# Attention and feed-forward on one core: value products in bursts, three shared PSUM buffers, and transposes on PE straight from the loaded rows

## The chip, the cores and the metric

The kernel runs on one core of a Trainium2 chip. The metric is the device time in microseconds (us), median of several runs. Engines: PE multiplies matrices, DVE (VectorE) and ACT (ScalarE) do elementwise work, POOL and SP mostly issue DMAs.

## The reference, cut to what matters

```python
# q, k, v: (8, 12, 448, 64)   w_in: (768, 2048)   w_out: (2048, 768)
scores = q @ k.T / sqrt(64)                  # for each batch and head
attn   = maximum(scores, 0) ** 2 / 448
x      = (attn @ v), heads side by side      # (8*448, 768)
out    = gelu(x @ w_in) @ w_out              # exact gelu
```

There is no softmax: each score tile goes through ReLU and a square, then into the value products. The first feed-forward layer is called F1 below and the second F2. Four heads are a "quad"; three quads make a batch.

## The kernel before

The core of attention: a score step fills one of two PSUM buffers (two banks each), ACT empties it, DVE squares it, and a value step accumulates into two further banks, which the quad holds from its first value step to its last copy.

```python
s_pp = pool("s_pp", 2, PS); av_pp = pool("av_pp", 2, PS); f_pp = pool("f_pp", 2, PS)

def qk_step(b, g, i):                        # 4 matmuls, 64x64 tiles, 448 columns
    ps = s_pp.tile([128, 2, NB], F32, tag="s", name="ps")
    ...
    nc.scalar.activation(ar, ps[:, :, :S], AF.Relu, scale=c_att)
    nc.vector.tensor_mul(a2, ar, ar)

def av_step(b, g, i):                        # 4 matmuls; i of 7 steps
    if i == 0:
        pav[b, g] = [av_pp.tile([128, NB], F32, tag="av", name="pav") for j in range(2)]
    ...
    if i == NK - 1:
        for j in range(2):
            nc.vector.tensor_copy(xT[b][:, 2 * g + j, :], pav[b, g][j][:, :S])
```

Rows of q and k have to be transposed before they can be multiplied. Batches 0 to 2 are first permuted by DVE, then transposed by PE; later batches are permuted by DVE and transposed by DMA. The tiles that hold the loaded rows (`nq`, `nk`) have one buffer each, so a batch can be loaded only when the one before it has been read.

```python
def transpose_dma(b):
    for w in (1, 0):
        ...
            nc.sync.dma_start_transpose(get_T(b)[w][:, :, off : off + r], perm[b][w][:r, t, :])

for b in range(2, B):                        # steady part
    ...
    if b == 2:
        prep[2] = [later(quad_T, 2, 1)]      # batch 2's quads: transposes on PE
        prep[6] = [later(quad_T, 2, 2)]
    if b + 1 < B:
        nxt = [later(permute_k, b + 1), later(permute_q, b + 1), later(transpose_dma, b + 1)]
    l = 10 if b == 2 else 2
    prep[l] = nxt
    if b + 2 < B:
        prep[l + 8] = [later(load, b + 2, 0, G)]
    weave(todo, atoms, prep)                 # two score steps, two value steps, some F1/F2
```

## Time and profile before

| | before |
|---|---|
| time, median of 3 | 423.77 us |
| span of the profiled run | 421.0 us |
| PE, DVE, ACT busy | 94%, 44%, 51% |
| first F1 product | 41.25 us |
| first F2 product | 87.99 us |
| from the last F2 product to the end | about 5 us |

### The profile page before, as it was taken

The page shows a single profiled execution, that of the slowest core. Times are in us where ns is not written, and L with a number is a line of the kernel's source. Part 1 is how long each engine was busy: PE and PEld are TensorE (multiplying, and loading weights), DVE is VectorE, ACT ScalarE, POOL GpSimd, SP SyncE. Part 2 cuts the span into 40 slices and gives each one's busy share as a digit, 9 for nine tenths or more (in the row PEclk, how much of TensorE's full clock was granted, in tenths as well). Part 3 has the DMA queues.
Part 4 walks back from the last instruction along what each step waited for, and adds up shares of the span by engine and source line. Part 5 has one row for each costly group of instructions (what it writes and reads, how often), then busy time and mean ns, then how long its engine had stood idle before and what let it go on. Part 6 is the DMA issues. An engine that isn't in the chain of part 4 may idle for free.

```text
span 421.0 us, 7489 instructions
## 1 busy us (share of the span) xinstructions
PE 395.6 (94%) x3152; PEld 200.8 (48%) x3152; DVE 186.1 (44%) x330; ACT 213.3 (51%) x302; POOL 60.9 (14%) x94
## 2 busy tenths in 40 slices
PE   2958998999989999999999999999999999999995
PEld 1323444554545545545445455545455455555562
DVE  1776656336446444464455443463453543300121
ACT  4875665654553556456564565465564654223200
POOL 8363060404104100050005000000000000000000
PEclk9998999999999999999999999999999999999998
DMA  9999399974995990199516990162011111001122
GB/s 141 159 156 200 63 164 209 205 117 78 174 191 85 172 173 15 39 140 166 99 37 92 179 174 2 39 142 66 2 37 39 39 37 29 24 26 37 39 75 75
DMA packets 68417, 41.41 MB, mean 98 GB/s; under 512 B 36640, under 2 KB 64800, under 8 KB 68384
## 3 DMA queue, kind: packets, MB, share of 16 engines
q0 software_dynamic: 35280, 22.58, 38.7%
q1 hardware_dynamic: 33104, 18.36, 22.3%
q8 instruction: 24, 0.39, 0.4%
q14 instruction: 9, 0.07, 0.1%
HBM read 45.61 MB, written 11.01 MB: 135 GB/s over the span
## 4 chain that ended last, share of the span: by engine, by line
PE 87%; DVE 5%; ACT 4%; issue 2%; DMA 1%; POOL 0%; ACTq 0%; DVEq 0%; POOLq 0%
PE pso L227 35%; PE psh L211 34%; PE pav L192 9%; PE ps L172 7%; ACT a_relu L180 4%; PE tp L144 2%; DVE a_sq L182 2%; DMA nk<-in_k_dram 1%; DVE xT L203 1%; DVE qT L150 1%; DVE kT L150 0%; DVE pk L132 0%; DVE pq L126 0%; POOL nk L79 0%; DVE osb L235 0%
## 5 line engine op out<-in xcount | busy, mean ns | idle before, releaser
L180 ACT ACTIVATE a_relu<-ps 128x896 bf16<-128x896 f32 x168 | 144.7, 916 | 116.6 <-PE ps L172 116.6
L211 PE MATMUL psh<-xT,win_sb 128*128 128x448 bf16 x768 | 156.6, 353 | 0.0
L227 PE MATMUL pso<-wout_sb,h_sb 128*128 128x384 bf16 x896 | 152.8, 326 | 0.0
L182 DVE TENSOR_TENSOR a_sq<-a_relu 128x896 bf16<-128x896 bf16 x168 | 104.4, 624 | 91.0 <-ACT a_relu L180 90.6
L227 PEld LDWEIGHTS <-h_sb 128*128 128x128 bf16 x896 | 86.3, 98 | 63.1 <-issue 5.9
L211 PEld LDWEIGHTS <-win_sb 128*128 128x128 bf16 x768 | 70.5, 98 | 79.4 <-issue 19.7
L218 ACT ACTIVATE h_sb<-psh 128x448 bf16<-128x448 f32 x128 | 70.0, 547 | 60.9 <-PE psh L211 60.9
L235 DVE COPY osb<-pso 128x384 f32<-128x384 f32 x56 | 31.2, 558 | 110.3 <-PE pso L227 110.3
L192 PE MATMUL pav<-a_sq,v_sb 64*64 64x448 bf16 x672 | 53.8, 370 | 10.0 <-DVE a_sq L182 5.2
L172 PE MATMUL ps<-qT,kT 64*64 64x448 bf16 x672 | 51.9, 368 | 4.1 <-ACT a_relu L180 2.8
L203 DVE CAST xT<-pav 128x448 bf16<-128x448 f32 x48 | 27.7, 619 | 16.2 <-PE pav L192 16.2
L192 PEld LDWEIGHTS <-v_sb 64*64 64x64 bf16 x672 | 16.3, 107 | 38.7 <-issue 36.9
L79 POOL DMA_DIRECT2D nk<-in_k_dram x12 | 9.4, 783 | 149.8 <-DVE pk L133 139.3
L89 POOL DMA_DIRECT2D v_sb<-in_v_dram x48 | 29.0, 628 | 14.3 <-DMA nk<-in_k_dram 8.9
L172 PEld LDWEIGHTS <-kT 64*64 64x64 bf16 x672 | 21.2, 108 | 20.6 <-issue 9.3
L144 PE MATMUL tp<-ident,pq 112*128 112x112 bf16 x72 | 6.2, 241 | 5.6 <-ACT pq L329 5.6
L83 POOL DMA_DIRECT2D nq<-in_q_dram x11 | 9.5, 859 | 0.7 <-DMA nk<-in_k_dram 0.5
L132 DVE COPY pk<-nk 128x768 bf16<-128x768 bf16 (+1 forms) x14 | 7.1, 510 | 5.4 <-DMA nk<-in_k_dram 5.4
L144 PE MATMUL tp<-ident,pk 128*128 128x128 bf16 x72 | 8.6, 232 | 0.4 <-DVE pk L132 0.4
L80 POOL DMA_DIRECT2D nk<-in_k_dram x12 | 8.4, 703 | 3.5 <-DMA win_sb<-in_moe_w_in_dram 3.5
L144 PEld LDWEIGHTS <-pk 128*128 128x128 bf16 x72 | 5.5, 101 | 5.5 <-DVE a_sq L182 1.2
L144 PEld LDWEIGHTS <-pq 112*128 112x128 bf16 x72 | 4.5, 112 | 7.4 <-ACT pq L329 5.6
(18 smaller groups left out, 32.8 us busy)
## 6 DMA issues: line engine op xcount, KB each, us to landing
v_sb<-in_v_dram POOLq DMA_DIRECT2D x48, 112.0 KB, 13.6
nq<-in_q_dram POOLq DMA_DIRECT2D x6, 672.0 KB, 14.8
win_sb<-in_moe_w_in_dram POOLq DMA_DIRECT2D x4, 768.0 KB, 10.2
wout_sb<-in_moe_w_out_dram POOLq DMA_DIRECT2D x2, 1536.0 KB, 16.9
out_dram<-osb SPq DMA_DIRECT2D x8, 336.0 KB, 2.8
nk<-in_k_dram POOLq DMA_DIRECT2D x6, 384.0 KB, 7.1
out_dram<-osb SPq DMA_DIRECT2D x8, 288.0 KB, 2.6
out_dram<-osb SPq DMA_DIRECT2D x8, 240.0 KB, 2.8
```

Source lines behind the costliest of these rows:

```text
L83: nc.gpsimd.dma_start(nq[b][:, h0:h1, :], qq)
L89: nc.gpsimd.dma_start(vt[b][64 * j : 64 * j + 64, g], vv[g, j])
L144: nc.tensor.transpose(tp[:, j, off : off + r], perm[b][w][:r, t, bass.ts(2 * g + j, 128)], ident[:r, :r],)
L172: nc.tensor.matmul(ps[64 * j : 64 * j + 64, e, :S], kT[r, 2 * g + j, kcol(i) : kcol(i) + KB], qT[r, 2 * g + j, :], start=True, stop=True,)
L180: nc.scalar.activation(ar, ps[:, :, :S], AF.Relu, scale=c_att)
L182: nc.vector.tensor_mul(a2, ar, ar)
L192: nc.tensor.matmul(pav[b, g][j][64 * e : 64 * e + 64, :S], vt[b][r, g, e, bass.ts(i, D)], a2[r, e, :], start=(i == 0), stop=(i == NK - 1),)
L203: nc.vector.tensor_copy(xT[b][:, 2 * g + j, :], pav[b, g][j][:, :S])
L211: nc.tensor.matmul(ph[:, :S], win_sb[:, kd, bass.ts(m, 128)], xT[b][:, kd, :], start=(kd == 0), stop=(kd == KD - 1),)
L218: nc.scalar.activation(hT[b // 2][:, m, (b % 2) * S : (b % 2 + 1) * S], ph[:, :S], AF.Gelu)
L227: nc.tensor.matmul(po[:, :ND], hT[pr][:, kf, bass.ts(t, 128)], wout_sb[:, kf, bass.ts(n, ND)], start=(kf == 0), stop=(kf == KF - 1),)
L235: nc.vector.tensor_copy(osb[:, bass.ts(n, ND)], po[:, :ND])
```

## The change

The intent: fewer changes between attention and feed-forward on PE, and an earlier start. The value products of a quad run as one burst of 28 matmuls; scores and values share three PSUM buffers of two banks; batches 0 to 2 are transposed by PE straight from the loaded rows, without DVE's permutation. With this come a planner that fixes each engine's order of work from estimated durations, batch 0 in two halves of q, ReLU on ACT or DVE while the first two batches run, and dummy matmuls at the start. Cut to its core:

```diff
-    s_pp = pool("s_pp", 2, PS)
-    av_pp = pool("av_pp", 2, PS)
+    w_pp = pool("w_pp", 3, PS)
     f_pp = pool("f_pp", 2, PS)
...
+        def fn(e_):                                   # values of one quad
+            pav.append(w_pp.tile([128, 2, NB], F32, tag="w", name="pav"))
+            for i, x in enumerate(blocks):            # 7 steps x 4 matmuls, one burst
...
+        def fn(e):                                    # transposes of k, no permutation
+            for i in range(NK):
+                for e in range(2):
+                    nc.tensor.transpose(
+                        tp[64 * e : 64 * e + 64, bass.ts(i, 128)],
+                        nk[b][:, 2 * g + e, bass.ts(i, D)], ident)
...
+            op = sch.add((("SP", 0.9, 12.0),), fn, [Pk[b, g]] + ...)  # DMA transpose, as planned
...
+    def slots(todo, first):                           # AV + 2 QK, or 3 QK, per slot
+            slot, room = [], first if not out else 3
...
+    for _ in range(SPIN):                             # SPIN = 45 dummies
+        nc.tensor.matmul(spin[:, 0, :128], zero, zero, start=True, stop=True)
...
+    add_win(0)
+    add_q(0, 0, G, HC, NC)                            # second half of q, batch 0
+    add_win(1)
...
+    add_steps(halves(0), dve=True)
...
+            n = per * (b - 2) + (6 if b == 2 else 0)  # copies of batch b + 1: after slot n
+            add_pk(b + 1, 0, G, after=at(n))
+            add_pq(b + 1, 0, G, after=at(n))
+            add_T_dma(b + 1, ...)
...
+    prep = {1: t2[1], 4: t2[2]}                       # batch 2's quads 1 and 2: slots 1 and 4
+    pe_q.extend(t2[0])
```

## The prediction

> **What bounds the kernel now.** I first read busy time by stretch, cutting where the work changes: the load, attention of batch 0 alone (to 41 us), attention of batch 1 with the first feed-forward products (to 78), the steady mixture (to 361), feed-forward alone. Columns: us, PE, PEld, DVE, ACT, POOL busy (instructions), clock, DMA share, GB/s.
>
> ```profile
> 0.00:6.00 6.00, 0.37 (x5) 0.37 (x6) 0.12 (x2) 2.53 (x3) 4.90 (x12) 1.00 0.75 137
> 6.00:20.00 14.00, 11.36 (x99) 4.76 (x96) 8.17 (x19) 9.65 (x12) 6.51 (x11) 1.00 1.16 162
> 20.00:41.00 21.00, 14.25 (x174) 6.42 (x173) 16.07 (x32) 14.07 (x17) 10.90 (x17) 0.92 1.20 171
> 41.00:78.00 37.00, 33.79 (x300) 16.35 (x293) 21.75 (x44) 24.64 (x36) 12.62 (x18) 1.00 0.97 155
> 78.00:361.00 283.00, 281.08 (x2269) 141.67 (x2267) 131.00 (x220) 153.75 (x219) 25.98 (x38) 1.00 0.59 93
> 361.00:421.00 60.00, 54.80 (x324) 31.23 (x320) 8.97 (x16) 8.70 (x16) 0.00 (x0) 0.98 0.16 46
> ```
>
> After 78 us PE never rests (281.08 of 283.00), and DVE and ACT are half idle: only PE's own work counts there. Before 41 us all engines have gaps: a chain of waits. Busy is not work, so I took PE's costs from its timeline (starts, not durations, as the ends are modelled):
>
> ```profile
> 162.04 3.58 PE L211 MATMUL psh<-xT,win_sb 128*128 128x448 bf16 x18
> 165.55 0.57 PE L192 MATMUL pav<-a_sq,v_sb 64*64 64x448 bf16 x8
> 165.95 0.55 PE L172 MATMUL ps<-qT,kT 64*64 64x448 bf16 x8
> 166.44 2.77 PE L227 MATMUL pso<-wout_sb,h_sb 128*128 128x384 bf16 x16
> ```
>
> And from the end of the chain that ended last:
>
> ```profile
> 390.46 4.54 PE psh L211 x24
> 395.00 20.81 PE pso L227 x128
> ```
>
> A first-layer product (call it F1) takes 4.54/24 = 0.189 us, a group of six 1.135; a second-layer product (F2) 20.81/128 = 0.1626, a group of sixteen 2.60. Four 64x64 products run together: eight score products take two passes of 0.189. From 165.55 to 165.95 is 0.40, so values to scores is nearly free. From 162.04 to 165.55 is 3.51 for 18 x 0.189 = 3.40: 0.11 of switching into attention; 165.95 to 166.44 is 0.49 for 0.38: 0.11 out of it. A visit to attention costs 0.22.
>
> The early part is told by its timeline:
>
> ```profile
> 11.35 0.59 PE L172 MATMUL ps<-qT,kT 64*64 64x448 bf16 x4 [0.22 <-ACT a_relu L180]
> 24.11 0.38 PE L192 MATMUL pav<-a_sq,v_sb 64*64 64x448 bf16 x2 [0.15 <-DVE xT L203]
> 26.49 0.38 PE L172 MATMUL ps<-qT,kT 64*64 64x448 bf16 x4 [0.23 <-ACT a_relu L180]
> 31.10 0.38 PE L192 MATMUL pav<-a_sq,v_sb 64*64 64x448 bf16 x2 [1.80 <-DMA win_sb<-in_moe_w_in_dram]
> ```
>
> ```profile
> 24.71 5.78 ACT L180 ACTIVATE a_relu<-ps 128x896 bf16<-128x896 f32 x7 [1.57 <-PE ps L172]
> ```
>
> Scores have two PSUM buffers, and ReLU on ACT alone empties them: seven in 5.78, one per 0.81. PE waits for it in each step; at each quad's end it waits for the copies xT, since the two value buffers are both held. No F1 can run before 41.25, when all three quads of batch 0 are done.
>
> **What the Trainium skill says.** "TensorE: Matmul & The Clock Gate", section Back-to-back issue gap, gives N/2.4 + 2.5 ns: for 448 columns 189.2 ns, for 384 162.5. The trace agrees (189, 162.6). Its section Part 1: The HAM clock gate says that an idle array runs at half rate until some 3.4 us of activity. The trace agrees: score passes show 0.59 at 11.35 and 0.38 at 26.49, with the transition near 19 us. "TensorEngine Tiling (Array Packing)", section Key Properties: "Changing tiling mode (not just tile) drains the TensorE". This fits the 0.11 us. Its section PSUM Bottleneck advises both ScalarE and VectorE for emptying PSUM; that the trace of before cannot show for ReLU, as ACT does all of it.
>
> **The change, part by part.** First the check of the method. From 79.1 us, where batch 1's first F1 group ends, to the last F2 at 415.8, PE has 111 F1 groups (126.0), 56 F2 groups (145.7), 250 attention passes (47.2), three quads of transposes at 1.3 (3.9): 322.8. The rest, 13.9, is 63 visits x 0.22, and the timeline shows about that many. So there is no other loss to win there.
>
> 1. Steady part. 21 score steps and three value bursts per batch become eight slots of three units (a seven-pass burst plus two score steps, or three score steps): 8 x 6 = 48 visits in place of 63. This saves 15 x 0.22 = 3.3 us. No matmul is removed. A slot carries about 4.5 us of feed-forward; three ReLUs take 2.5 of ACT and about three Gelus of 0.55 take 1.6, so ACT should stay hidden, narrowly. From the boundary T0 (attention of batches 0 and 1 and F1 of batch 0 done) the changed PE needs 112 x 1.135 = 127.1, + 145.7, + 252 x 0.189 = 47.6, + 3.9, + 48 x 0.22 = 10.6: 334.9 us. T0 in before is about 77.6.
>
> 2. Start. DVE's permute copies before the transposes of batches 0 to 2 go (about 0.4 + 0.2 + 0.4 us a quad, of which some 0.7 was on the path before the first score). The first k comes by a hardware queue rather than behind the POOL issue (first k copy at 6.33), and half of q comes first. I expect the first ReLU at about 7.8 us instead of 9.57. Dummy matmuls warm the clock, so the 0.59 passes go: about 7 us of PE work was at half rate, worth perhaps 2 to 3 us, as PE was partly waiting.
>
> 3. Batch 0 in halves of q, so F1 on half the rows starts before the other half. Half 0 is 11 score tiles. By tile: ReLU 0.81 on ACT, square 0.54 pitch on DVE; plus six copies of transposes (4.5 full ones x 0.54) and six half copies xT of 0.3: 14.9 + 2.4 + 1.8 = 19.1 us, on two engines 9.6. From 7.8: 17.4, plus the last values and copies: F1 starts at 19, not 41.25.
>
> 4. ReLU may go to DVE: 896 elements at the xT rate (448 in 0.54 pitch) are about 1.0 us. All post-processing of batches 0 and 1: 43 ReLUs 34.8 and 16 Gelus 7.8 on ACT, 43 squares 23.2, copies 14.2 on DVE: 80 us, balanced 40 per engine. So it ends near 48 to 52.
>
> 5. PE to T0: transposes of six quads at 1.3: 7.8; 84 passes 15.9, + 0.3 for halves; F1 18.2, + 0.6 for 224 columns at 2.5 ns more each; 25 visits x 0.22 = 5.5. Sum 48.3. With the first transpose at 5.5, some 3.5 us idle before 19 and 2 later, T0 = 59.3.
>
> 6. Loads: page GB/s peaks at 205 to 209, counted in bf16. Batches 0 and 1 (4.1 MB) and the first weights (3.1 MB) are 7.2 MB: 36 us from about 2.5, so near 40. The second weights come after batch 2: 5.2 MB more, 65 us. F2 is first wanted about 13 us after T0, so the loads are just in time.
>
> The largest of PE 59, post-processing 52, loads 42 is T0. Span = 59.3 + 334.9 + 5.2 (the last copy and store, 415.8 to 421.0, unchanged) = 399.4. The timed runs lie 2.8 above the span (423.8 against 421.0): 402; I shade it to 401, as post-processing overlaps and fewer visits may occur early.
>
> **Rivals.** (a) PE transposes become dearer. They double in number: 14 for k and 16 for q per quad, 64 columns wide, against 16. If two 64-column tiles don't overlap, 30 x 0.075 = 2.25 us rather than 1.3, over nine quads + 8.6: 408 to 410. Against: score tiles with different columns do overlap; for: they use all 128 rows each.
> (b) The loads set T0. Against: peak rate ends them at 40; for: the page shows 141 to 159 in the first slices, and single buffers of q and k let batch 1 load only after batch 0's transposes. Then T0 = 65, and F2 waits too: 408.
> (c) Post-processing binds steadily: three ReLUs in a row delay Gelu and with it the two feed-forward buffers. If each of 48 slots loses 0.25 us, + 12: 413. For: ACT is in order and F1 waits on only two buffers; against: ACT is 54% busy after 78 us.
> (d) Everything early packs well and visits are few: T0 = 50, set by post-processing: 392.
> (e) Nothing gained at the start since ACT remained the bound: only 3.3 us, 420. Against: 25 of PE's first 41 us lie idle or at half rate, and half the DVE was free.
>
> **Range and chances.** Between (d) and (b) lies most: predicted 401 us, range 392 to 411. "Faster by over 2%" needs 415.3; only (c) or (e) with others miss it: 0.95. Within 2% 0.04, slower 0.01.
>
> **What would show it.** First F1 near 19 us (wrong if after 26). F2 first near 70 to 75. T0 near 59. No score pass at 0.59 after the first few. In the steady part, PE idle under 3 us, 48 visits, value bursts of 28 in about 1.35 us. From the first score of batch 2 to the last F2, 335 us; if this is over 342, (c) holds. A quad's transposes near 1.3 us; at 2.2, (a). PE waiting for DMA before 60 us by more than 4 us: (b). A result outside 392 to 411 means that T0 or the steady sum is wrong by more than 9 us.

## The result, and the profile after

The changed kernel took 421.93 us (420.82 to 422.48, 4 runs) beside 423.92 us for the kernel before (4 runs). The ratio is 0.9953, interval 0.9928 to 0.9977: the same within 2%. A ratio here is the mean time of one kernel's runs over that of the other's of the same rounds, so it isn't quite the ratio of the medians. The predicted 401 us was 21 us too low.

Busy time of each engine in the same stretches as before (columns as there):

```profile
0.00:6.00 6.00, 4.01 (x45) 3.84 (x45) 0.82 (x4) 1.98 (x3) 4.87 (x11) 1.00 0.68 166
6.00:20.00 14.00, 9.80 (x216) 7.74 (x218) 10.65 (x18) 8.20 (x12) 6.63 (x10) 0.79 1.35 176
20.00:41.00 21.00, 18.48 (x368) 14.63 (x369) 17.95 (x28) 17.06 (x29) 16.28 (x24) 0.90 1.14 154
41.00:78.00 37.00, 35.55 (x443) 23.74 (x436) 21.18 (x34) 24.86 (x41) 9.68 (x14) 1.00 1.05 170
78.00:361.00 283.00, 270.60 (x2214) 140.56 (x2211) 117.52 (x223) 154.35 (x231) 12.94 (x15) 0.98 0.58 91
```

The early stretches improved: PE is busy for 18.48 us between 20 and 41, where it was 14.25. The loss is in the stretch which I had called free of waits: from 78 to 361 PE now rests for 12.4 us, and it did for 1.9 before. The waits of the changed kernel name one cause (engine, line, released by: us in total, times, longest):

```profile
PE ps L457 <- DMA qT<-pq: 12.3, 1, 12.3
```

It happened once. PE's timeline around it:

```profile
107.87 2.44 PE L563 MATMUL psh<-xT,win_sb 128*128 128x448 bf16 x12
110.25 1.52 PE L516 MATMUL pav<-a_sq,v_sb 64*64 64x448 bf16 x28
124.03 0.96 PE L457 MATMUL ps<-qT,kT 64*64 64x448 bf16 x8 [12.26 <-DMA qT<-pq]
124.92 7.91 PE L603 MATMUL pso<-wout_sb,h_sb 128*128 128x384 bf16 x32
```

The first scores of batch 3 wait for q and k transposed by DMA. The wait costs more than its 12.3 us: the 32 F2 products after it take until 132.75, 7.8 us where 5.2 is normal, since the granted clock had fallen during the idle time (0.50 of full from 118 us). Behind the wait stands a chain, which POOL's, DVE's and SP's timelines show (issue of the load of batch 3's k; DVE's copy of it; the DMA transposes of k and of q as issued from SP):

```profile
90.95 0.82 POOL L291 DMA_DIRECT2D nk<-in_k_dram  x1 [37.49 <-PE tp L374]
```
```profile
102.09 0.99 DVE L327 COPY pk<-nk 128x896 bf16<-128x896 bf16 x3
```
```profile
102.58 6.44 SPq L423 DMA_TRANSPOSE kT<-pk  x3
109.12 12.18 SPq L431 DMA_TRANSPOSE qT<-pq  x4
```

POOL waited 37.49 us before that load, for PE's transposes of batch 2: the last quad of batch 2 is transposed in slot 4, at 90 us, and only then is the single buffer free. From there: load 11 us, copies, then seven DMA transposes whose issue alone lasts from 102.58 to 121.30, and the last landing at 123.9. PE had reached batch 3 at 111.8. Shortly before, from 75 to 90 us, the DMA engines had done almost nothing (DMA share 0.09):

```profile
75.00:90.00 15.00, 15.00 (x121) 7.91 (x119) 5.41 (x9) 7.54 (x12) 0.00 (x0) 1.00 0.09 27
```

One more thing may stretch the chain. Beside these seven transposes runs the load of batch 4, which POOL issues from 103.37 us. They take 21.3 us from the first issue to the last landing. The seven of the last batch, with no load beside them, take 11.7 us, to 278.6:

```profile
266.89 5.00 SPq L423 DMA_TRANSPOSE kT<-pk  x3
271.99 5.21 SPq L431 DMA_TRANSPOSE qT<-pq  x4
```

So the load beside them may account for much of the wait. No run held it back, so this stays untested.

The kernel before has nearly the same chain. Its transposes for batch 3 were issued from 100.39 to 119.33 too. But there batch 3 began only at 124.09, since batch 2 had begun 10 us later (75.22 against 65.56). In the kernel before:

```profile
100.39 6.04 SPq L156 DMA_TRANSPOSE kT<-pk  x4
106.48 12.85 SPq L156 DMA_TRANSPOSE qT<-pq  x4
```
```profile
124.09 0.57 PE L172 MATMUL ps<-qT,kT 64*64 64x448 bf16 x8
```

The last of these was issued at 117.1 and landed 6.5 us later, at 123.6: the slack was half a microsecond, and no wait showed it. The faster start brought PE to a deadline that had not moved.

### The profile page after: what moved, and what is told of

Read it like the earlier page. It is cut to its first block, busy times and chain, and to the rows that moved or that the text cites. A ratio compares the mean times of both kernels' runs of the same rounds, so it can differ in the third digit from the quotient of the medians.

```text
span 420.0 us, 8294 instructions
## 1 busy us (share of the span) xinstructions
PE 392.6 (93%) x3587; PEld 221.3 (53%) x3587; DVE 176.6 (42%) x321; ACT 215.2 (51%) x328; POOL 50.4 (12%) x72
## 4 chain that ended last, share of the span: by engine, by line
PE 84%; DMA 7%; POOL 3%; SPq 2%; ACT 1%; DVE 1%; issue 1%; POOLq 0%; ACTq 0%
PE pso L603 36%; PE psh L563 33%; PE ps L457 7%; PE pav L516 7%; DMA nq<-in_q_dram 4%; SPq L431 2%; DMA nk<-in_k_dram 2%; DMA qT<-pq 1%; PE tp L399 1%; POOL v_sb L306 1%; ACT a_relu L469 1%; POOL nq L206 1%; POOL win_sb L223 1%; POOL nk L291 0%; POOL win_sb L224 0%
## 5 line engine op out<-in xcount | busy, mean ns | idle before, releaser
L469 ACT ACTIVATE a_relu<-ps 128x896 bf16<-128x896 f32 x155 | 136.4, 917 | 62.9 <-PE ps L457 61.8
L563 PE MATMUL psh<-xT,win_sb 128*128 128x448 bf16 (+1 forms) x864 | 156.6, 332 | 0.0
L479 DVE TENSOR_TENSOR a_sq<-a_relu 128x896 bf16<-128x896 bf16 (+1 forms) x169 | 103.1, 621 | 93.5 <-ACT a_relu L469 93.3
L563 PEld LDWEIGHTS <-win_sb 128*128 128x128 bf16 x864 | 80.6, 98 | 68.6 <-issue 13.9
L457 PE MATMUL ps<-qT,kT 64*64 64x448 bf16 (+1 forms) x756 | 46.7, 342 | 15.9 <-DMA qT<-pq 12.3
L516 PE MATMUL pav<-a_sq,v_sb 64*64 64x448 bf16 (+1 forms) x756 | 39.0, 346 | 0.8 <-ACT a_relu L469 0.8
L259 ACT CAST xT<-pav 128x448 bf16<-128x448 f32 (+1 forms) x36 | 16.8, 482 | 37.2 <-PE pav L516 37.2
L257 DVE CAST xT<-pav 128x448 bf16<-128x448 f32 (+1 forms) x18 | 10.8, 599 | 34.6 <-ACT xT L259 34.5
L471 DVE TENSOR_SCALAR a_relu<-ps 128x896 bf16<-128x896 f32 x14 | 15.2, 1085 | 1.9 <-PE ps L457 1.7
L306 POOL DMA_DIRECT2D v_sb<-in_v_dram x14 | 10.7, 761 | 2.8 <-DMA win_sb<-in_moe_w_in_dram 2.0
```

The source lines that it names most:

```text
L257: V.tensor_copy(dst, src)
L259: A.copy(dst, src)
L457: nc.tensor.matmul(ps[64 * j : 64 * j + 64, e, x * w : x * w + w], kT[r, g, i * 128 + 64 * j : i * 128 + 64 * j + 64], qT[r, 2 * g + j, co ...
L469: A.activation(ar, ps, AF.Relu, scale=c_att)
L471: V.tensor_scalar(ar, ps, c_att, 0.0, op0=mybir.AluOpType.mult, op1=mybir.AluOpType.max,)
L479: V.tensor_mul(box["a2"][:, :, :used], ar, ar)
```

## The experiments

The theory, A: two gates in a row, late transposes of batch 2 (hence the late load) and copies ordered late on DVE, make batch 3 late, and this one wait hides the gain. Rivals: B, DMA transposes are too slow wherever they start; C, other losses come out once the wait is gone; D and E, only one of the two gates matters (D the order of the copies, E the late load). For the 4 us that my T0 was off, F (order of loads) and H (half-rate clock). Runs of different calls were on different chips, where the kernel before took 423.6 to 424.5 us, so I compare ratios to before.

| run | time, us | ratio to before | interval |
|---|---|---|---|
| e1_both_early | 406.0 | 0.9580 | 0.9560 to 0.9599 |
| e2_gate_early | 419.6 | 0.9901 | 0.9875 to 0.9927 |
| e3_t2_early | 422.0 | 0.9958 | 0.9931 to 0.9984 |
| e4_pe_batch3 | 411.9 | 0.9707 | 0.9678 to 0.9736 |
| s1_q_first | 403.5 | 0.9506 | 0.9477 to 0.9535 |
| s2_slots12 | 417.9 | 0.9838 | 0.9798 to 0.9878 |
| s3_relu_act | 403.9 | 0.9518 | 0.9489 to 0.9547 |
| s4_no_halves | 415.2 | 0.9779 | 0.9748 to 0.9810 |
| s5_warm | 408.6 | 0.9624 | 0.9596 to 0.9652 |
| s6_nospin | 405.6 | 0.9547 | 0.9512 to 0.9583 |
| s8_q_first_slow | 403.1 | 0.9503 | 0.9470 to 0.9534 |
| s9_combo | 404.0 | 0.9518 | 0.9485 to 0.9550 |

All gave correct results.

### e1_both_early: both gates opened

```diff
-    prep = {1: t2[1], 4: t2[2]}
-    pe_q.extend(t2[0])
+    prep = {}
+    pe_q.extend(t2[0] + t2[1] + t2[2])
...
-            n = per * (b - 2) + (6 if b == 2 else 0)
+            n = per * (b - 2) + (3 if b == 2 else 0)
```

> Theory A (late chain): the one PE stall of 12.3 us in the changed kernel comes because the third quad of batch 2 is transposed only at 90 us, so batch 3 is loaded only from 91 us (q and k have one buffer), copied at 102 and transposed by DMA until 124, while PE runs dry at 111.8. With all three quads transposed at once (near 64 to 67 us) and the copies ordered three slots earlier, the load should issue near 68 us, land near 80, the DMA transposes end near 105. Stall under 1 us, no half-rate products after it: 420 - 12.3 - 2.6 = 405 us span, 407 timed. Rival B (DMA transposes too slow whatever their start, or they collide with the second weights): the stall stays above 6 us and the time above 415. Rival C (the stall hides other losses, which return as waits elsewhere): stall gone, time still above 412.

Measured: 406.0 us, span 403.6. The same three places in its timelines, POOL, SP and PE:

```profile
66.50 0.82 POOL L291 DMA_DIRECT2D nk<-in_k_dram  x1 [12.97 <-PE tp L374]
```
```profile
81.93 5.59 SPq L423 DMA_TRANSPOSE kT<-pk  x3
```
```profile
110.50 0.57 PE L457 MATMUL ps<-qT,kT 64*64 64x448 bf16 x8
111.01 5.37 PE L603 MATMUL pso<-wout_sb,h_sb 128*128 128x384 bf16 x32
```

The load starts 24 us sooner, the transposes 21 us, and PE goes from batch 2 to batch 3 without a wait; the F2 products after it take 5.3 us again. No matmul was removed or added, and the span fell by 16.4 us. This is theory A with the forecast's size (405 span), and it rules out B and C: the DMA transposes are no quicker (issued from 81.93 to 101.0), they merely have the time.

### e2_gate_early and e3_t2_early: one gate each

```diff
# e2: only the copies earlier
-            n = per * (b - 2) + (6 if b == 2 else 0)
+            n = per * (b - 2) + (3 if b == 2 else 0)
# e3: only batch 2's transposes earlier
-    prep = {1: t2[1], 4: t2[2]}
-    pe_q.extend(t2[0])
+    prep = {}
+    pe_q.extend(t2[0] + t2[1] + t2[2])
```

> Half of the repair: only the copies and DMA transposes of batch 3 are ordered earlier; batch 2 is still transposed late. Theory A: the load still issues near 91 us, k lands near 99 and q near 102.5, so only some 3 us are won: stall 8 to 11 us, time 417 to 420. If the order of the copies on DVE were the cause (rival D), the stall would go: 407.

> The other half: batch 2 transposed at once, so that the load issues near 68 us, but the copies of batch 3 stay behind the sixth slot in DVE's order, near 102 us. Theory A in its full form (two gates in a row, both near 102 us): stall stays at 10 to 13 us, time 420 to 423, although the data lie in the buffer since 80. If the late load alone were the cause: 407.

DVE's first copy of batch 3's k and PE's wait, first in e2, then in e3:

```profile
97.61 0.99 DVE L327 COPY pk<-nk 128x896 bf16<-128x896 bf16 x3
```
```profile
123.27 0.96 PE L457 MATMUL ps<-qT,kT 64*64 64x448 bf16 x8 [11.21 <-DMA qT<-pq]
```
```profile
101.18 0.98 DVE L327 COPY pk<-nk 128x896 bf16<-128x896 bf16 x3
```
```profile
123.97 0.96 PE L457 MATMUL ps<-qT,kT 64*64 64x448 bf16 x8 [13.12 <-DMA qT<-pq]
```

Both as expected. In e2 the load still issues at 90.42; k can be copied 4 us sooner, q not until 101.20, and 1.1 us of the wait goes. In e3 the load issues at 66.76 and the data lie ready, but DVE's order holds the copy until 101.18, and nothing is won. Neither gate alone is the cause, so D and E fall: 420 and 422 with one, 406 with both. An engine's fixed order is a gate like a semaphore, though no wait names it.

### e4_pe_batch3: the DMA transposes taken out of the path

```diff
+            if b == 2:
+                t3 = [[add_tk(3, g), add_tq(3, g)] for g in range(G)]
+            else:
                 ... add_pk, add_pq, add_T_dma as before
...
-    prep = {1: t2[1], 4: t2[2]}
+    prep = {1: t2[1], 4: t2[2], 8: t3[0] + t3[1] + t3[2]}
```

> Batch 3 is transposed by PE from its loaded rows, as batches 0 to 2 are; batch 2 still late. Load lands near 102 to 103 us, before PE asks for batch 3 near 111. Theory A: the stall goes but PE pays three quads of transposes, 3 x 1.2 = 3.6 us, and the wait for their copies, about 1 us: 405 + 4.6 = 410 us span, 412 timed. If the load and not the DMA transposing were the longer part (rival E), PE would wait for it by over 4 us. A second stall at batch 4, whose load now waits for these transposes, is possible: load from 113, copies near 126, DMA transposes until 146, wanted near 156, so I expect none.

Measured: 411.9 us, span 410.2. PE at the start of batch 3 (first lines of its transposes, and the burst that follows them):

```profile
110.92 0.58 PE L374 MATMUL tp<-ident,nk 128*64 128x128 bf16 x14
114.89 1.52 PE L516 MATMUL pav<-a_sq,v_sb 64*64 64x448 bf16 x28
```

Three quads cost PE 3.97 us with their small waits, and the 12 us wait is gone although the load was as late as in the changed kernel (issued at 91.63). So the load alone was in time; it is the load and the 21 us of DMA transposing together that were not. E falls again.

### s1_q_first: what is left at the start

From here on each edit is made on top of e1.

```diff
-    add_win(0)
     add_q(0, 0, G, HC, NC)
+    add_win(0)
```

> On top of the repaired kernel (both early). What is left of my error lies before T0 (63.0 us measured, 59.3 forecast). Theory F (load order): PE's fixed order puts batch 0's second-half transposes at 15.7 us, but that half of q lands only at 17.3 and later, behind the first chunk of weights; everything behind it waits, and batch 1's q load too. Loading that half before the weights should bring T0 to 60 to 61.5 and the time from 406.0 to 403.5 to 405. Theory H (half-rate clock between 8 and 27 us is the cause): T0 stays within 0.7 us and the time within 1 us of 406.0.

In the changed kernel PE waits for the second half of q, which was issued behind the first chunk of weights:

```profile
17.32 0.86 PE L399 MATMUL tp<-ident,nq 112*64 112x112 bf16 x16 [1.60 <-DMA nq<-in_q_dram]
```

In s1:

```profile
15.13 1.65 PE L399 MATMUL tp<-ident,nq 112*64 112x112 bf16 x24 [0.72 <-DMA nq<-in_q_dram]
```

All of batch 0's transposes are then done before 17 us rather than after 20, and batch 1's q load issues at 17.35 instead of 20.78 in e1. F1 of batch 0 ends at 61.30 instead of 63.02. The time is 403.5 us: 2 to 3 us less (medians 406.0 and 403.5, ratios 0.9580 and 0.9506). Theory F holds for about 2 of the 4 us.

### s5_warm and s6_nospin: the clock at the start

```diff
# s5: ten dummies ahead of each score tile of batch 0's first half
+                for _ in range(warmup):
+                    nc.tensor.matmul(ps[:, 0, :128], zero, zero, start=True, stop=True)
# s6
-SPIN = 45
+SPIN = 1
```

> On top of the repaired kernel: ten dummy products of 128 columns before each of the eleven score tiles of batch 0's first half (5.9 us of dummy work at full rate), to hold the clock up between 8 and 25 us, where value bursts of 28 took 1.45 us rather than 0.72. Theory H: the doubled passes vanish, F1 starts 2 us sooner or more, and the time falls to 403 to 405. Theory F (PE waits for loads and copies there, its speed matters little): no gain, 405.5 to 409, as the dummies themselves come in the way.

> On top of the repaired kernel: one dummy product at the start instead of 45, all else the same instructions in the same order. My prediction gave the dummies 2 to 3 us. If the granted clock falls back at about 10 us anyhow and only the first transposes and scores gain (some 1.5 us of PE work before the first ReLUs), the time rises by 0.3 to 1.5 us: 406.3 to 407.5. If they are worth what I said: 408 to 409. If nothing on the path: 406.0.

s5 is slower than e1 (0.9624 against 0.9580), and F1 starts at 31.68 us instead of 27.09. It is not a clean test of the clock. The dummies took room on PE, and the clock fell all the same soon after PE had waited for q; two lines of s5, the wait and a tile after it:

```profile
17.24 0.58 PE L399 MATMUL tp<-ident,nq 112*64 112x112 bf16 x16 [2.96 <-DMA nq<-in_q_dram]
20.05 0.59 PE L461 MATMUL ps<-qT,kT 64*64 64x224 bf16 x8
```

So what the half rate between 10 and 27 us costs by itself stays open. s6 is clear: without the dummies at the start the time is 405.6 (0.9547, interval overlapping that of e1). They are worth nothing that these runs can resolve.

### s2_slots12: the price of a visit

```diff
-            slot, room = [], first if not out else 3
+            slot, room = [], 2
...
-    per = 8
+    per = 12
```

(The copies of batch 3 come after slot 5, to stay in proportion.)

> On top of the repaired kernel: slots of two units rather than three, so 12 visits to attention per batch instead of 8. It tests step 1 alone: 24 more visits x 0.22 = 5.3 us: 411.3 us timed. Rival: visits cost less than the timeline says because they hide something (two ReLUs in a row suit ACT better than three): 408 or less. The waits on PE should stay under 3 us in the steady part in either case.

Measured: 417.9 us (415.5 to 419.8), and in the profiled run a span of 415.8, that is 12.2 us over e1's instead of 5.3. A part is a fault of the experiment: batch 3 was late again, by 3.86 us, and the F1 products after it ran at half rate.

```profile
112.71 0.59 PE L457 MATMUL ps<-qT,kT 64*64 64x448 bf16 x4 [3.86 <-DMA qT<-pq]
113.23 3.81 PE L563 MATMUL psh<-xT,win_sb 128*128 128x448 bf16 x12
```

The stretch from the first score of batch 5 to the first of batch 7 is undisturbed in both: 208.23 to 302.37 us here, 202.82 to 295.12 in e1. That is 94.14 against 92.30 us for the same products, with 24 visits instead of 16: 0.23 us a visit, where the prediction read 0.22. For the profiled runs the sum closes: 24 x 0.23 = 5.5, wait 3.9, half-rate 1.5, a start 1.2 us later: 12.1 of 12.2.

### s3_relu_act and s4_no_halves: two parts of the early stage

```diff
# s3: ReLU on ACT alone
-    add_steps(halves(0), dve=True)       ... and the same for steps(1)
+    add_steps(halves(0))
# s4: batch 0 in whole rows, F1 of batch 0 too
-    add_steps(halves(0), dve=True)
+    add_steps(steps(0), dve=True)
...
-        add_f1(0, m, 0, bias=F1_BIAS)    ... and the loop for the second half
+        add_f1(0, m, bias=F1_BIAS)
```

> On top of the repaired kernel (406.0): no ReLU on DVE; the 14 that DVE took before 54 us go to ACT, 14 x 0.81 = 11.3 us more there. Step 4 of the prediction: ACT then has some 43 us of early work plus its copies from 8.8 us on, ending near 54 to 56, close under T0 (63): F1 starts some 2 us later, the time rises by 1 to 3 us, 407 to 409. Rival: T0 is set by PE alone, no change (within 1 us).

> On top of the repaired kernel: batch 0 in whole rows, so that its F1 can start only after all of its attention, near 33 to 36 us instead of 27 to 28. Step 3: PE then has no feed-forward to fill its waits before that; it loses most of the roughly 7 us shift: 410 to 414 us. Rival: batch 1's attention fills the gap as well as F1 does: 406 to 408.

s3 was a miss: I expected a loss and it is faster than e1, 403.9 us, 0.9518 against 0.9580. A ReLU on DVE takes 1.08 us, one on ACT 0.81 in a row, and ACT had room. In its trace batch 0's last transposes and the load of batch 1's q come 1.6 us sooner (19.14 us against 20.78), so it may have gained the way s1 did; s9 tests this.

s4 costs 8.4 us against e1 by the ratios, more than expected, so the halves are worth most of the start. But it overstates their worth. Since s4 scores whole rows, its first score needs the second half of q as well, and waits for it:

```profile
17.14 1.66 PE L399 MATMUL tp<-ident,nq 112*64 112x112 bf16 x24 [5.53 <-DMA nq<-in_q_dram]
46.31 1.31 PE L563 MATMUL psh<-xT,win_sb 128*128 128x448 bf16 x6
```

F1 starts at 46.31, even later than in the kernel before (41.25).

### s8_q_first_slow and s9_combo: the best version

```diff
# s8: s1, and the planner's loads slower
-            self.dma = t + lat[0] / (300e3 if t < 10 else 390e3)
+            self.dma = t + lat[0] / (250e3 if t < 10 else 350e3)
# s9: s8 and s3 together
```

> Candidate for the best: repaired, second half of q before the weights (403.5), and the planner that fixes each engine's order told that loads are slower (250 and 350 kB per us of source data instead of 300 and 390), since PE's order put transposes ahead of loads that had not landed. If the order is what costs PE its last early waits for loads (some 3 us before 41): 401.5 to 403. If it merely trades them for idle slots: 403 to 405.

> The best candidate: batch 2 transposed at once and batch 3 copied early, second half of q loaded before the weights, planner told of slower loads, all ReLUs on ACT. The run without ReLU on DVE gained 2 us where the forecast was a loss; its trace shows batch 0's last transposes at 17 to 18.5 us instead of near 20, and batch 1's q load issued at 19.1 instead of 20.8. If that gain came from the same load order that the q-first run repaired (theory F), the two do not add: 402 to 404. If DVE's 1.08 us ReLUs in themselves cost time (they hold up squares, theory G), they add: 400 to 401.5.

s8 is at 403.1 us (0.9503), not to be told from s1. s9 is at 404.0 (0.9518): the gains of s1 and s3 do not add, as they should not if both come from batch 0's transposes, and thus the next load, being done sooner. That fits theory F and speaks against G (DVE's ReLUs in themselves cost time), but as the planner reorders all engines in each of these runs, it isn't proof. Another reading is open: s9's F1 starts at 23.38 us, sooner than s8's (25.13), but PE then waits 1.1 us for DVE's copies of kT among batch 2's transposes, a wait that s8 does not have. The best are s1 and s8, near 403 us: 5% under the kernel before and 4.5% under the changed kernel (0.9503/0.9953).

## Why the prediction was wrong, point by point

The forecast span was 399.4 us, the measured one 420.0. Of the 20.6 us between them, 12.3 are the wait for batch 3, about 3.1 the half-rate products after it (2.6 for F2, 0.5 for scores), and 4.3 a later T0 (63.6, not 59.3). That leaves 0.9. One reading was wrong without doing harm: the timed runs lie about 2 us above their own spans (422.99 against 421.0 in the profiled run of before), not 2.8. So the sum meant 401.4 rather than 402, and shading it to 401 was luck.

**The step that failed is 6, loads:** "F2 is first wanted about 13 us after T0, so the loads are just in time." It added up bytes and divided by the peak rate. Bytes were not the limit, with the DMA engines nearly idle from 75 to 90 us (share 0.09). What counted was a chain of dependences: the last reader of a single buffer, the load, the copies, the DMA transposes. I did name the single buffers, in rival (b), but only for batch 1; and for the steady part I wrote "there is no other loss to win there" without asking what a sooner PE would run into. The DMA transposes of batch 3, in plain sight in the trace of before (issued from 100.39 to 119.33, batch 3 begun at 124.09), stood in no term of the sum. With a slack of half a microsecond there, a start that is 10 us sooner had to meet them. The planner makes the same mistake: it books a DMA transpose with 0.9 us of issue and 12 us to the end, and the trace shows 1.2 to 4.6 us of issue each, one after the other.

**Step 1 was right.** e1 needs 340.6 us from the end of batch 0's F1 (63.0) to the end of its span (403.6); the forecast was 334.9 + 5.2 = 340.1. From batch 3's first score to batch 7's the kernel before took 186.92 us with 42 visits, e1 184.62 with 32: 0.23 a visit. Rival (c), ACT delaying Gelu, did not happen: e1's PE is busy for all of 78 to 361 us. The prediction's sign for (c), over 342 us from batch 2's first score to the last F2, did come in the changed kernel (65.56 to 415.1, 350 us), but for the other reason: the sign could not tell a wait for ACT from one for a DMA.

**Step 2 was wrong in size.** The first ReLU came at 9.16 us, not 7.8. The dummies did not do away with passes at half rate: a burst of 28 at 18.48 us still took 1.45 us of PE's time, twice its warm cost, and s6 shows no gain from them. The trace of before had warned of it: there the full rate came only near 19 us, 13 us after PE's first product (5.63), and the 0.59 passes are back at 34.26. It agreed with the two rates, but not with the 3.4 us of activity that the prediction cites; that stage is full of waits.

**Step 3 was right in kind, wrong in size.** F1 started at 28.68, not 19 (before: 41.25). I left out that PE's order is fixed: a transpose whose q hasn't landed holds up scores that could run. But that is a small part of the ten us: where this wait is 0.7 us (s1) and 0.4 (s8), F1 still starts at 26.48 and 25.13. The rest stays open. s4 shows that the halves matter, by at most 8 us.

**Step 4 was wrong:** ReLU on DVE won nothing (s3). Balance between the two engines was not the limit in these runs.

**Step 5, T0,** was 4.3 us short. s1 shows that the order of loads accounts for about 2; the clock's share stays open (s5). (The 0.6 us for 224 columns is 0.24 by its own figure: 96 more products at 2.5 ns.) The price of the transposes was right: e1 takes 3.8 us for three quads (63.02 to 66.84), so rival (a) is out, the pairs of 64-column tiles do overlap.

## What to carry to other kernels

A faster stage moves every later consumer forward; before counting the gain, list what each of them needs next and how much slack that chain has in the trace now, even if no wait shows there today. A chain through a single buffer begins at its last reader, so look whether that reader can be moved forward: here the last quad of transposes came 24 us sooner, at no cost in work. When two gates lie in a row, opening one shows little (0 to 2 us here, 16 with both), so test both together before dropping the theory.

## What the Trainium skill lacked or had wrong

- "DMA: Bandwidth & Descriptors", section DMA Transpose (X-bar), gives constraints but no measured time for a batch of small transposes between SBUF tiles issued from one queue. Here seven of them (1.38 MB, worked out from their shapes) took 18.7 us to issue, 1.3 to 4.1 us each, and 21.3 us to land, beside a load: some 65 GB/s. The last batch's seven, with no load beside them, took 10.3 us to issue and 11.7 to land: some 118 GB/s. Its section Latency and other measured facts states 261 GB/s as effective for DMA_TRANSPOSE in one measured case, which no run here approached.
- "TensorEngine Tiling (Array Packing)", section Key Properties, says that changing the tiling mode drains the engine, but has no figure: entering 64x64 products and leaving them again cost 0.23 us, by two differences between three kernels (before, e1, s2). That the drain is what costs it, no run shows.
- "TensorE: Matmul & The Clock Gate", section Part 1: The HAM clock gate, gives some 3.4 us of activity until the full rate is back. After the 12.3 us wait the granted clock was 0.50 from 120 to 130 us, so PE worked at half rate for about 6 us (from 124.03), and the 40 products after the wait took 3.1 us more than elsewhere. (The page also calls the window free-running, which may account for the difference; no run tests it.) Its section Part 4: PE-mode transpose, says that the full clock does not engage for transposes; here a quad's 14 transposes of k took 0.58 us where the clock was up (1.00, at 63.56 us of the changed kernel) and 0.96 where it was down (0.50, at 25.72), so among other products they run at the granted clock. Whether transposes alone would raise it, no run shows.
